# Queries' scores in partition order, the last chunk's stores from two queues, and a list order made anew, in a pack-attention and two-layer kernel on one Trainium2 core

## The chip, the core and the metric

The kernel runs on one core of a Trainium2 chip (trn2). The core has five engines that work side by side, each through its own list of instructions in order: TensorE (PE in the profile; PEld is its loading of weights), VectorE (DVE), ScalarE (ACT), GpSimd (POOL) and SyncE (SP), which here only issues DMA transfers. An engine that reaches an instruction whose input is not ready waits, and everything behind it in its list waits too. The metric is the device time of one execution in microseconds; less is better.

## The reference

Two attentions, then two dense layers. Inputs of the attention are q, k, v of shape (8 batches, 8 heads, 576 rows, 64) and p of shape (8, 8, 32, 64), float32.

```python
def sm_attn(qq, kk, vv):
    s = scale * np.matmul(qq, kk.transpose(0, 1, 3, 2))
    s = s - np.max(s, axis=-1, keepdims=True)
    a = np.exp(s)
    a = a / (np.sum(a, axis=-1, keepdims=True) + 1e-09)
    return np.matmul(a, vv)
p_packed = sm_attn(p, k, v)
x = sm_attn(q, p_packed, p_packed)      # then to (4608 tokens, 512)
# first layer (w_in 512x2048, w_out 2048x512, float64)
h = x @ w_in
P = a[0] + a[1] * h + a[2] * h**2 + a[3] * h**3
Q = 1.0 + abs(b[0]) * abs(h) + abs(b[1]) * h**2
x = ((P / (Q + 1e-6)) @ w_out).astype(np.float32)
# second layer, with its own w_in and w_out
h = x @ w_in
out = ((h * np.cos(h)) @ w_out).astype(np.float32)
```

The four weight matrices come as float64.

## The kernel before

**Attention.** The work is cut into 16 units u, one batch and four heads each. For each unit SyncE loads p, k, q and v (`load`); TensorE transposes k and q (`trans`), makes the first scores (`scores` with k = 0, L497), and after `max1`, `exp1`, `turn_exp` and `pack` the second scores, those of the queries against the packed rows (`scores` with k = 1). The second softmax runs on VectorE, GpSimd and ScalarE: `turn2` (a transpose, L581), `max2`, `less_max2`, `exp2`, `sum2`, `recip2`, `scaled2`, `turn_back` (L608). `keep_attn` (L611) stores the unit's result, the tile a2T, to DRAM from SyncE. A query's row number is 18 x partition + column; `of_head` reads the transposed columns, and for the queries it permutes them (index j, a), so that the tokens of a unit stand in blocks of 96 rows. `store` undoes this permutation at the very end through `cols_of`.

**First layer.** 128 items j, in 16 chunks of 8 items; a chunk c is 288 tokens. Ahead of each chunk its operand is loaded from DRAM (`a2_load`, SyncE), rounded to a high half (`a2_hi`, ScalarE, L684) and a low half (`a2_lo`, GpSimd, L687): the float32 products are made of three products of such halves. `m_load` and `m_prod` (L691) merge the packed rows with w_in into the operand M of a batch, split by `m_hi` (ScalarE) and `m_lo` (VectorE). An item is `front` (12 matmuls, L733, rows L743), the rational function in ten steps on ScalarE, VectorE and GpSimd (`absolute`, `lin`, `slope`, two `cubic` (L854, L856), `denom` on GpSimd (L866, rows L868), `rsqrt`, `square`, `over`, `ratio`), the splitting of its result into gh (`upper`, ScalarE) and gl (`lower`, VectorE), and `back` (L764, rows L780), four pieces that add into the accumulators.

**Second layer.** 144 items in 9 chunks of 512 tokens with 16 items each, the same shape with a cosine in place of the rational function. Its weights are converted while the first layer runs. At a chunk's end `done2` (L794) copies the four accumulator tiles out, two on ScalarE and two on VectorE, and `store` (L801) sends each tile to DRAM in four stores of 32 rows of 2 KB, all issued by SyncE.

**Weights.** float64 is turned into float32 by bit operations (`convert`, L405): `w_load` on SyncE into one of two buffers called raw, `w_exp` and `w_low` on ScalarE (L362), `w_abs` and `w_join` on VectorE (L381), and for most a split `w_hi` (ScalarE) and `w_lo` (GpSimd, L393). `w_in` of the first layer comes in 16 slabs f, `w_load(0, f, i)`; `m_prod` reads slabs 0 to 7 for its first half and 8 to 15 for its second.

**What sets the order.** No instruction's place is written by hand. While the program is built, the class Plan gets every step with an engine, an estimated duration and a key (about the time at which it should run), shifted by the number for its kind in the table WANTED. `Plan.order` (L118) walks through a made-up time, lets DMA transfers share one bus of RATE bytes per ns, and picks on each engine the step with the least key among those that could begin soon. The list that results for each engine is then fixed (`manual_schedule`). The keys of the attention come from FROM + u x UNIT, those of the first layer's conversions from a line in the item number. So one number in these tables can move instructions on every engine.

Of the kernel before, what the change touches and what calls it, by code (L numbers as in the profile page):

```python
# [27 lines left out]
class Plan:  # L28
# [11 lines left out]
    WINDOW = 60  # L40

    WANTED = {
        "a2_hi": 425, "a2_lo": 322, "a2_load": -80, "absolute": -759, "back 0": 65, "back 1": 130,
        "clipped": 158, "copied k": 134, "copied q": -49, "cosine": 272, "cubic 0": 306,
        "cubic 1": -373, "denom": -204, "done1": -251, "done2": -15, "doubled": 206, "exp1": 136,
        "exp2": -30, "exp_copied 0": -90, "exp_copied 1": 531, "front 0": -349, "front 1": -353,
        "keep_attn": 269, "keep_out": 130, "keep_pack": 152, "less_max2": -482, "lin 0": -197,
        "lin 1": -324, "load k": 278, "load p": -295, "load q": -297, "load v": 153, "lower 0": -68,
        "lower 1": 31, "m_hi": -104, "m_lo": -5, "m_load": -283, "m_prod": -385, "max1": -518,
        "max2": -130, "open_left": -238, "open_right": 397, "over 0": 48, "over 1": 82, "pack": 387,  # L50
        "packed": -296, "ratio": 12, "recip1": 167, "recip2": 132, "reduced 0": 243,
        "reduced 1": -199, "rounded": 269, "rsqrt": 244, "scaled2": 33, "scores 0": -163,
        "scores 1": 165, "slope": -174, "square": -374, "store": 310, "sum2": -42, "taken p": -65,
        "taken pp": 152, "times": -67, "trans k": 216, "trans q": 121, "turn2": 62,
        "turn_back": -264, "turn_exp": 97, "turned p": 95, "turned pp": 513, "upper 0": -254,
# [6 lines left out]
        "x_load": -108, "x_out": -463,  # L62
    }
    RATE = 275.0
    SHARED = ("over", "ratio", "lower", "rounded", "clipped", "w_abs", "w_join", "x_lo")

    def __init__(self, slots, mixed):
# [134 lines left out]
def pack_attention_moe_moe_kernel(  # L202
# [14 lines left out]
    nc = tc.nc  # L217
    B, H, S, D = q.shape
# [3 lines left out]
    P = 128  # L222
    KC = DM // P
    NF = FF // P
    CH = 512
    NCH = NT // CH
    TP = 96
    TCN = S // TP
    HS = S // 2
    N3 = TCN // 2  # L230
    NJ = TP // 32
    NT9 = S // 64
    G4 = 4
# [75 lines left out]
    add = plan.add  # L309
    TILE = {}  # L310
# [13 lines left out]
    par = POOL["cp"].tile([P, 8], F32, name="par")  # L324
    cst = POOL["cp"].tile([P, 4], F32, name="cst")

    def cols_of(i):
        return 2 * (i % N3) + i // N3

    def halves_of(t):  # L330
        return t[:, 0:CH], t[:, CH : 2 * CH]

# [143 lines left out]
        t0, t1 = PIECES[j]  # L476
        nc.scalar.copy(TILE[nm + "T", u][:, t0 * P : t1 * P], piece(u, nm, j))

    def of_head(t, h, k):

        if k == 0:
            return t.rearrange("q (t h p) -> q t h p", t=NT9, h=G4)[:, :, h, :]
        return t.rearrange("q (j a h p) -> q a j h p", j=NJ, a=N3, h=G4)[:, :, :, h, :]

    def doubled(u):
        t = TILE["p", u]
# [10 lines left out]
    def scores(u, k, lhs, rhs):  # L497

        for e in range(2):
            rows = slice(e * D, (e + 1) * D)  # L500
            for h in range(G4):
                r = slice(h * NP, (h + 1) * NP)
                nc.tensor.matmul(  # L503
                    TILE["s", u, k][r, e, 0:HS],
                    lhsT=TILE[lhs, u][rows, r],
                    rhs=of_head(TILE[rhs, u][rows], h, k),
                    start=True,
                    stop=True,
                )
# [101 lines left out]
    def keep_attn(u):  # L611
        nc.sync.dma_start(a2[u], TILE["a2T", u])

    UNIT, FROM = 30.47, -351.0
    exps, ld_users, tp_users, ps_users = [], [], [], []

    def attention(u):
# [180 lines left out]
        else:  # L798
            nc.scalar.copy(ob, acc)

    def store(c, m):  # L801
        ob = TILE["o", c, m]
        a, e = c * CH + m * P, c * CH + (m + 1) * P
        while a < e:
            blk, p0 = divmod(a, TP)
            b, i = divmod(blk, TCN)
            jj, p0 = divmod(p0, 32)
            n = min(e - a, 32 - p0)
            rows = out[b * S : (b + 1) * S, :].rearrange("(p j c) d -> j p c d", j=NJ, c=TCN)
            o = a - (c * CH + m * P)  # L810
            nc.sync.dma_start(rows[jj, p0 : p0 + n, cols_of(i), :], ob[o : o + n, :])
            a += n

    def x_pieces(c):
        done = 0
# [126 lines left out]
    t = add("-", 0, 0, open_right, after=tp_users)  # L942
    OPEN |= dict.fromkeys(("gp", "op", "xp", "wo1", "aps"), t)

    for n in range(0, NF, NF // 2):
        for e, which in enumerate("io"):
            for f in range(n, n + NF // 2):
                convert(0, f, which, -1257.8 + 36.58 * (f + n + e * NF // 2))

    ps2 = ([P, 2, CH], F32)  # L950
    W2P = ([P, 2 * HS], F32)
# [2 lines left out]
    for f in range(NF // 2, NF):  # L954
        part, e = divmod(f - NF // 2, 2)
        a, g = divmod(part, NG)
# [67 lines left out]
    def item2(j):  # L1024
        l, c, f = items[j]
        key = at(j)
        fronts[j] = add("PE", 2775, key, front, j, tail=170, r=[("win2", f), *(("x", c, kk) for kk in range(KC))], new=[("b2", ("h", j), *ps2)], after=[fronts[j - 1]] if j else ())
        add("ACT", 520, key, lin, j, tail=100, r=[("h", j)], new=[("T", ("T", j), *W2P)])
        add("DVE", 336, key, rounded, j, tail=85, w=[("T", j)])
        add("DVE", 605, key, reduced, j, 0, tail=85, r=[("T", j), ("h", j)], new=[("U", ("U", j), *W2P)])  # L1030
        add("DVE", 605, key, reduced, j, 1, tail=85, r=[("T", j)], w=[("U", j)])
        add("DVE", 336, key, clipped, j, tail=85, w=[("U", j)])
        add("ACT", 535, key, cosine, j, tail=100, w=[("U", j)], after=rsqrts[-8:] if j < N1 + 8 else ())
        add("DVE", 600, key, times, j, tail=85, r=[("U", j), ("h", j)], new=[("V", ("V", j), *W2P)])
        add("ACT", 510, key, upper, j, tail=100, r=[("V", j)], new=[("gh", ("gh", j), [P, 2 * HS], F32R)])
        add("DVE", 600, key, lower, j, tail=85, r=[("V", j), ("gh", j)], new=[("gl", ("gl", j), [P, 2 * HS], F32R)])
        for m in range(KC):
            home = dict(w=[("acc", 1, c, m)]) if f else dict(new=[("acc", ("acc", 1, c, m), [P, CH], F32)])
            add("PE", 694, key, back, j, m, tail=170, r=[("gh", j), ("gl", j), ("wo", 1, f)], **home)
        if f == NF - 1:  # L1040
            for m in range(KC):
                add("DVE" if m % 2 else "ACT", 510 + 90 * (m % 2), key - 30, done2, c, m, tail=90, r=[("acc", 1, c, m)], new=[("sc" if m < 3 else "xr", ("o", c, m), [P, CH], F32)])
                add("SP", 300, key, store, c, m, r=[("o", c, m)], kb=256)

    KEEP1, KEEPN = 14, 6.2
    for c in range(NH):
# [69 lines left out]
```

## Time and profile before

| | us |
|---|---|
| median of three runs (1689.8 to 1692.67) | 1690.48 |
| the profiled execution | 1691.2 |
| its span | 1689.4 |
| TensorE busy (94% of the span) | 1579.6 |
| loading of weights, PEld (80%) | 1347.9 |
| VectorE busy (76%) | 1289.7 |
| ScalarE busy (60%) | 1020.5 |
| GpSimd busy (18%) | 310.4 |
| DMA queue q1, 119.06 MB | 23.9% of 16 engines' span |

The mean granted clock of TensorE was 0.972. The attention fills roughly the first 200 us, the first layer lasts until about 880 us and the second until the end. A busy share is a mean over these stages; where the time is lost has to be read stage by stage, from windows and from the timeline.

### The profile page before, as it was taken

What the parts mean: (1) busy time and instruction counts of PE and PEld (TensorE: products, weight loads), DVE (VectorE), ACT (ScalarE), POOL (GpSimd) and SP (SyncE); (2) the same over time, 40 slices, a digit from 0 to 9 for tenths busy, and PEclk for the clock granted to TensorE, in tenths of its full rate; (3) what the DMA queues carried; (4) which work ended last, traced back from release to release, by engine and by line L of the source; (5) the groups of instructions that cost most, each with busy time, mean ns of one, the idle gap of its engine ahead of it and who ended that gap; (6) DMA issues with size and microseconds to landing.
All of it is one profiled execution on the core that took longest, in us unless ns stands there. A gap on an engine that the chain in (4) does not pass through costs nothing.

```text
span 1689.4 us, 26694 instructions
## 1 busy us (share of the span) xinstructions
PE 1579.6 (94%) x10176; PEld 1347.9 (80%) x10176; DVE 1289.7 (76%) x2025; ACT 1020.5 (60%) x1706; POOL 310.4 (18%) x246
## 2 busy tenths in 40 slices
PE   5766488999999999999999999999999999999997
PEld 3444287999998999998998888888888888888886
DVE  2656888999988999989998866666676757576664
ACT  4656788989889999979886533333333333343332
POOL 0233333324333433333322100000000000000000
PEclk7988789999999999999999999999999999999999
DMA  9997431211211211213153210101010101001011
GB/s 262 252 285 223 123 106 44 66 50 53 69 47 56 66 50 53 69 47 134 55 185 86 79 44 7 38 13 38 13 38 11 36 5 31 20 17 34 1 25 26
DMA packets 84384, 120.76 MB, mean 71 GB/s; under 512 B 19232, under 2 KB 61216, under 8 KB 84256
## 3 DMA queue, kind: packets, MB, share of 16 engines
q1 hardware_dynamic: 84256, 119.06, 23.9%
q8 instruction: 80, 1.31, 0.3%
q14 instruction: 48, 0.39, 0.1%
HBM read 85.99 MB, written 33.03 MB: 70 GB/s over the span
## 4 chain that ended last, share of the span: by engine, by line
PE 79%; DVE 7%; ACT 7%; DMA 2%; issue 2%; POOL 1%; SPq 0%; ACTq 0%; POOLq 0%; DVEq 0%
PE acc L780 42%; PE b L759 24%; PE b L743 9%; PE b L471 1%; PE b L698 1%; PE b L503 1%; DMA v_in<-in_v_dram 1%; ACT T L845 1%; ACT V L859 1%; DVE T L879 1%; DVE T L854 1%; DVE U L879 1%; DVE gl L914 1%; PE one L554 1%; DVE T L856 1%
## 5 line engine op out<-in xcount | busy, mean ns | idle before, releaser
L780 PE MATMUL acc<-gh,wo 128*128 128x288 f32 x2048 | 418.2, 298 | 14.3 <-ACT gh L911 14.3
L780 PE MATMUL acc<-wo,gh 128*128 128x512 f32 x1152 | 359.1, 393 | 0.0
L780 PEld LDWEIGHTS acc<-gh,wo 128*128 128x128 f32 x2048 | 331.4, 189 | 33.1 <-ACT gh L911 18.9
L780 PE MATMUL acc<-gl,wo 128*128 128x288 f32 x1024 | 304.9, 298 | 6.9 <-DVE gl L914 6.8
L780 PEld LDWEIGHTS acc<-wo,gh 128*128 128x128 f32 x1152 | 216.2, 188 | 49.3
L868 POOL TENSOR_TENSOR U<-U,V 128x576 f32<-128x576 f32 x128 | 183.4, 1442 | 367.3 <-DVE T L883 76.8
L780 PE MATMUL acc<-wo,gl 128*128 128x512 f32 x576 | 226.6, 393 | 0.0
L902 ACT ACTIVATE U<-U 128x512 f32<-128x512 f32 x144 | 90.7, 630 | 196.0 <-DVE U L898 195.8
L780 PEld LDWEIGHTS acc<-gl,wo 128*128 128x128 f32 x1024 | 193.9, 189 | 8.9 <-DVE gl L914 8.9
L914 DVE TENSOR_TENSOR gl<-V,gh 128x512 fp32r<-128x512 f32 x144 | 100.0, 695 | 132.2 <-PE acc L780 131.0
L847 ACT ACTIVATE T<-b 128x512 f32<-128x512 f32 x144 | 85.9, 596 | 189.8 <-PE b L759 189.2
L911 ACT CAST gh<-V 128x512 fp32r<-128x512 f32 x144 | 89.3, 620 | 79.6 <-PE acc L780 76.8
L780 PEld LDWEIGHTS acc<-wo,gl 128*128 128x128 f32 x576 | 108.1, 188 | 24.9
L887 DVE TENSOR_SCALAR T<-T 128x512 f32<-128x512 f32 x144 | 62.2, 432 | 79.0 <-ACT T L847 78.9
L914 DVE TENSOR_TENSOR gl<-T,gh 128x576 fp32r<-128x576 f32 x128 | 106.6, 836 | 10.2 <-PE acc L780 4.3
L905 DVE TENSOR_TENSOR V<-U,b 128x512 f32<-128x512 f32 x144 | 98.4, 683 | 18.2 <-ACT U L902 14.3
L879 DVE SCALAR_TENSOR_TENSOR T<-T,par,V 128x576 f32<-128x576 f32 x128 | 104.8, 834 | 8.8 <-ACT V L875 8.5
L862 ACT ACTIVATE U<-V,par 128x576 f32<-128x576 f32 x128 | 110.9, 872 | 0.2
L845 ACT ACTIVATE T<-b,par 128x576 f32<-128x576 f32 x128 | 106.1, 834 | 2.1 <-DVE gl L914 1.7
L894 DVE SCALAR_TENSOR_TENSOR U<-T,U 128x512 f32<-128x512 f32 x144 | 103.5, 719 | 4.0
L854 DVE TENSOR_TENSOR T<-T,b 128x576 f32<-128x576 f32 x128 | 93.7, 745 | 16.5 <-ACT T L845 14.9
L856 DVE SCALAR_TENSOR_TENSOR T<-T,par,b 128x576 f32<-128x576 f32 x128 | 101.8, 810 | 3.9 <-ACT V L859 1.4
(182 smaller groups left out, 3055.8 us busy)
## 6 DMA issues: line engine op xcount, KB each, us to landing
raw<-in_moe_w_out_dram SPq DMA_DIRECT2D x32, 512.0 KB, 3.7
q_in<-in_q_dram SPq DMA_DIRECT2D x16, 576.0 KB, 5.2
k_in<-in_k_dram SPq DMA_DIRECT2D x16, 576.0 KB, 6.8
x<-ob SPq DMA_DIRECT2D x16, 576.0 KB, 3.4
raw<-in_moe_w_in_dram SPq DMA_DIRECT2D x32, 256.0 KB, 4.3
v_in<-in_v_dram SPq DMA_DIRECT2D x64, 128.0 KB, 5.1
raw<-in_moe_w_in_dram SPq DMA_DIRECT2D x16, 512.0 KB, 4.1
w<-sc SPq DMA_DIRECT2D x32, 256.0 KB, 2.4
```

The lines of the kernel that those rows point to most:

```text
L743: nc.tensor.matmul(TILE["h", j][:, e, 0:HS], lhsT=w[:, o : o + P], rhs=x[:, g, :], start=n == 0, stop=n == 3 * NG - 1,)
L759: nc.tensor.matmul(h, lhsT=w[:, ks], rhs=x, start=n == 0, stop=n == 3 * KC - 1)
L780: nc.tensor.matmul(o, lhsT=w, rhs=x, start=i == 0 and n == 0, stop=i == last and n == len(todo) - 1,)
L845: nc.scalar.activation(T, hidden(j), AF.Identity, scale=par[:, 3:4], bias=par[:, 2:3])
L854: nc.vector.tensor_tensor(T, T, h, op=ALU.mult)
L856: nc.vector.scalar_tensor_tensor(T, T, par[:, 1:2], h, op0=ALU.add, op1=ALU.mult)
L862: nc.scalar.activation(shaped(j, "U"), shaped(j, "V"), AF.Identity, scale=par[:, 5:6], bias=par[:, 4:5])
L868: return nc.gpsimd.tensor_tensor(Q, Q, V, op=ALU.mult)
L879: return nc.vector.scalar_tensor_tensor(t, t, add_, shaped(j, "V"), op0=ALU.add, op1=ALU.mult)
L894: return nc.vector.scalar_tensor_tensor(Y, T, -C2, Y, op0=ALU.mult, op1=ALU.add)
L905: nc.vector.tensor_tensor(shaped(j, "V"), shaped(j, "U"), hidden(j), op=ALU.mult)
L914: return nc.vector.tensor_tensor(shaped(j, "gl"), result(j), shaped(j, "gh").bitcast(F32), op=ALU.subtract)
```

## The change

Four edits.

1. **Order.** The table WANTED gets new numbers for nearly all kinds, RATE goes from 275 to 262, the keys of the attention units become -291.5 + 18.35 u (from -351 + 30.47 u), and those of the first layer's conversions start earlier and stand closer together. The planner is charged 450 ns for each store that is issued (before: 300 for the four of a tile together).
2. **Queries in partition order.** `of_head` drops the permutation: queries are read with the pattern that the keys had.
3. **Stores.** `store` gives rows in the new order, still four stores of 32 rows of 2 KB for a tile, 18 rows apart in the output; `cols_of` goes.
4. **Last chunk.** In the last chunk pieces 0 and 1 of each tile are issued by SyncE, pieces 2 and 3 by ScalarE, behind the copies that ScalarE makes there.

```diff
-        "a2_hi": 425, "a2_lo": 322, "a2_load": -80, "absolute": -759, "back 0": 65, "back 1": 130,
+        "a2_hi": 440, "a2_lo": 373, "a2_load": -22, "absolute": -628, "back 0": 104, "back 1": 169,
...
-    RATE = 275.0
+    RATE = 262.0
...
-    def of_head(t, h, k):
-
-        if k == 0:
-            return t.rearrange("q (t h p) -> q t h p", t=NT9, h=G4)[:, :, h, :]
-        return t.rearrange("q (j a h p) -> q a j h p", j=NJ, a=N3, h=G4)[:, :, :, h, :]
+    def of_head(t, h):
+        return t.rearrange("q (t h p) -> q t h p", t=NT9, h=G4)[:, :, h, :]
...
-    UNIT, FROM = 30.47, -351.0
+    UNIT, FROM = 18.35, -291.5
...
-    def store(c, m):
-        ob = TILE["o", c, m]
-        a, e = c * CH + m * P, c * CH + (m + 1) * P
-        while a < e:
-            blk, p0 = divmod(a, TP)
-            b, i = divmod(blk, TCN)
-            jj, p0 = divmod(p0, 32)
-            n = min(e - a, 32 - p0)
-            rows = out[b * S : (b + 1) * S, :].rearrange("(p j c) d -> j p c d", j=NJ, c=TCN)
-            o = a - (c * CH + m * P)
-            nc.sync.dma_start(rows[jj, p0 : p0 + n, cols_of(i), :], ob[o : o + n, :])
-            a += n
+    def store(c, m, queue, pieces):
+
+        for n in pieces:
+            b, a = divmod(c * CH + m * P + n * 32, S)
+            e, t = divmod(a // 32, NT9)
+            rows = out[b * S : (b + 1) * S, :].rearrange("(p t e) d -> e t p d", t=NT9, e=2)
+            queue.dma_start(rows[e, t], TILE["o", c, m][32 * n : 32 * (n + 1), :])
...
-                convert(0, f, which, -1257.8 + 36.58 * (f + n + e * NF // 2))
+                convert(0, f, which, -1473.7 + 32.65 * (f + n + e * NF // 2))
...
-                add("SP", 300, key, store, c, m, r=[("o", c, m)], kb=256)
+                ends = ((nc.sync, (0, 1)), (nc.scalar, (2, 3))) if c == NCH - 1 else ((nc.sync, range(4)),)
+                for queue, pieces in ends:
+                    eng = "SP" if queue is nc.sync else "ACT"
+                    add(eng, 450 * len(pieces), key, store, c, m, queue, pieces, r=[("o", c, m)], kb=256)
```

What the new numbers do to the lists, at three places. In these rows a line is that of its own version of the kernel, and the number behind a tile's name is a running one.

First, GpSimd's list around the low half of chunk 7's operand (`a2_lo(7)`, the row that writes a_1). U<-U,V is `denom` of one item each; before, these are the items 53, 54, 55, then 56 and 57. Chunk 7 begins with item 56. sc<-sc,sc is `w_lo` of the second layer. Before:

```order
L868 TENSOR_TENSOR U_5745<-U_5745,V_5739 128x576
L393 TENSOR_TENSOR sc_5802<-sc_5629,sc_5674 128x512
L868 TENSOR_TENSOR U_5781<-U_5781,V_5754 128x576
L868 TENSOR_TENSOR U_5833<-U_5833,V_5813 128x576
L689 TENSOR_TENSOR a_1_5694<-xr_5436,a_1_5694 128x576
L868 TENSOR_TENSOR U_5978<-U_5978,V_5966 128x576
L868 TENSOR_TENSOR U_5999<-U_5999,V_5987 128x576
```

After, with the items 48, 49, then 50 and 51:

```order
L390 TENSOR_TENSOR sc_5400<-sc_5241,sc_5300 128x512
L857 TENSOR_TENSOR U_5449<-U_5449,V_5443 128x576
L857 TENSOR_TENSOR U_5485<-U_5485,V_5458 128x576
L683 TENSOR_TENSOR a_1_5508<-xr_5422,a_1_5508 128x576
L857 TENSOR_TENSOR U_5538<-U_5538,V_5516 128x576
L857 TENSOR_TENSOR U_5605<-U_5605,V_5556 128x576
```

The low half stood behind denom(55), one item ahead of its chunk; it now stands behind denom(49). a2_lo(13) moves in the same way, from behind denom(103) to behind denom(97).

Second, SyncE's list where the attention ends. raw<-in_moe_w_in_dram is `w_load` of one slab of the first layer's w_in, here slabs 10 to 15 in order; a<-a2T is `keep_attn`, here of units 13, 14 and 15; pt<-ppt is `m_load`. Before:

```order
L345 DMA raw_2328<-in_moe_w_in_dram 64x512 x2
L345 DMA raw_2369<-in_moe_w_in_dram 64x512 x2
L612 DMA a_13_85<-a2T_2367 128x576
L345 DMA raw_2436<-in_moe_w_in_dram 64x512 x2
L345 DMA raw_2443<-in_moe_w_in_dram 64x512 x2
L673 DMA pt_2460<-ppt_90 128x128
L345 DMA raw_2484<-in_moe_w_in_dram 64x512 x2
L345 DMA raw_2498<-in_moe_w_in_dram 64x512 x2
L612 DMA a_14_86<-a2T_2505 128x576
L612 DMA a_15_87<-a2T_2511 128x576
```

After:

```order
L342 DMA raw_2340<-in_moe_w_in_dram 64x512 x2
L606 DMA a_13_85<-a2T_2352 128x576
L606 DMA a_14_86<-a2T_2373 128x576
L342 DMA raw_2407<-in_moe_w_in_dram 64x512 x2
L342 DMA raw_2413<-in_moe_w_in_dram 64x512 x2
L342 DMA raw_2454<-in_moe_w_in_dram 64x512 x2
L667 DMA pt_2472<-ppt_90 128x128
L342 DMA raw_2479<-in_moe_w_in_dram 64x512 x2
L606 DMA a_15_87<-a2T_2484 128x576
L342 DMA raw_2520<-in_moe_w_in_dram 64x512 x2
```

The stores of the units 13 and 14 now stand ahead of slab 11, and that of unit 15 ahead of slab 15; before, the units 14 and 15 came behind the last slab.

Third, ScalarE's list at the end. sc<-acc is `done2` of the tiles 0 and 2. Before, it ends so:

```order
L902 ACTIVATE U_16643<-U_16643 128x512
L911 CAST gh_16674<-V_16638 128x512
L911 CAST gh_16690<-V_16664 128x512
L799 COPY sc_16721<-acc_16227 128x512
L799 COPY sc_16735<-acc_16245 128x512
```

After:

```order
L793 COPY sc_16721<-acc_16227 128x512
L801 DMA out_dram<-sc_16721 32x512 x2
L793 COPY sc_16737<-acc_16241 128x512
L801 DMA out_dram<-sc_16730 32x512 x2
L801 DMA out_dram<-sc_16737 32x512 x2
L801 DMA out_dram<-xr_16741 32x512 x2
```

ScalarE issues two of the four stores of every tile, and those of tile 0 stand between its two copies.

## Rows read from the trace of the kernel before

**Rows 1.** The page: busy tenths of TensorE and DMA in 40 slices.

```profile
PE   5766488999999999999999999999999999999997
DMA  9997431211211211213153210101010101001011
```

**Rows 2.** Windows: us, PE busy (instructions), PEld, DVE, ACT, POOL, PEclk, DMA, GB/s.

```profile
500.00:510.00 10.00, 9.36 (x70) 9.12 (x69) 6.81 (x8) 7.24 (x12) 4.49 (x3) 1.00 0.00 0
...
500.00:600.00 100.00, 95.88 (x753) 90.97 (x759) 91.07 (x124) 89.99 (x145) 36.75 (x26) 1.00 0.16 52
600.00:700.00 100.00, 100.00 (x808) 94.14 (x788) 96.20 (x131) 92.29 (x148) 36.15 (x26) 1.00 0.18 58
700.00:800.00 100.00, 97.21 (x762) 91.78 (x761) 92.13 (x124) 85.88 (x136) 33.52 (x24) 1.00 0.27 91
1500.00:1600.00 100.00, 100.00 (x435) 81.17 (x434) 66.28 (x115) 35.59 (x61) 0.00 (x0) 1.00 0.07 16
```

**Rows 3.** Timeline, chunks 7 and 13: start, duration, engine, operation, [idle before <- releaser].

```profile
479.40 0.70 ACT L685 CAST a<-xr 128x576 fp32r<-128x576 f32 x1
...
499.58 2.03 POOL L689 TENSOR_TENSOR a<-xr,a 128x576 fp32r<-128x576 f32 x1 [4.21 <-DVE U L879]
...
501.67 0.40 PE L743 MATMUL b<-a,m00h 128*128 128x288 f32 x1 [0.64 <-POOL a L689]
...
749.00 2.03 POOL L689 TENSOR_TENSOR a<-xr,a 128x576 fp32r<-128x576 f32 x1 [6.02 <-issue]
...
778.12 0.50 PE L743 MATMUL b<-a,m10h 128*128 128x288 f32 x2 [1.47 <-DVE T L856]
```

**Rows 4.** Timeline, from attention to the first layer: VectorE, ScalarE and TensorE.

```profile
185.81 0.77 DVE L581 STREAM_TRANSPOSE r<-b 128x576 f32<-128x576 f32 x1
...
189.21 0.66 ACT L362 ACTIVATE sc<-raw 128x512 f32<-128x512 f32 x1
...
207.06 0.85 PE L780 MATMUL acc<-gh,wo 128*128 128x288 f32 x2 [12.61 <-ACT gh L911]
...
211.06 1.43 DVE L914 TENSOR_TENSOR gl<-T,gh 128x576 fp32r<-128x576 f32 x2 [1.34 <-DMA a<-a2T]
...
211.88 0.61 PE L780 MATMUL acc<-gl,wo 128*128 128x288 f32 x1 [3.97 <-DVE gl L914]
```

**Rows 5.** Timeline, same stretch: SyncE's DMA issues (SPq), slab 15's join, m_prod(0,1,1).

```profile
178.59 5.11 SPq L345 DMA_DIRECT2D raw<-in_moe_w_in_dram  x4
...
183.75 0.58 SPq L612 DMA_DIRECT2D a<-a2T  x1
...
206.91 1.86 SPq L612 DMA_DIRECT2D a<-a2T  x2
...
213.68 0.68 DVE L381 SCALAR_TENSOR_TENSOR s<-raw,sc 128x512 uint32<-128x512 uint32 x1
...
217.10 1.09 PE L698 MATMUL b<-s,pt 64*32 64x512 f32 x16
```

**Rows 6.** The end: a window, the timeline, all store issues (ns: least/median/most).

```profile
1679.30:1682.30 3.00, 1.43 (x7) 0.85 (x5) 1.38 (x2) 0.60 (x2) 0.00 (x0) 1.00 0.45 107
...
1679.34 5.87 SPq L811 DMA_DIRECT2D out_dram<-sc  x12
...
1680.09 0.59 ACT L799 COPY sc<-acc 128x512 f32<-128x512 f32 x1 [0.77 <-PE acc L780]
...
1680.77 0.69 DVE L797 COPY xr<-acc 128x512 f32<-128x512 f32 x1 [0.67 <-PE acc L780]
...
1685.31 1.79 SPq L811 DMA_DIRECT2D out_dram<-xr  x4
...
L811 SPq DMA_DIRECT2D out_dram<-sc x108: 314/423/823, 982.6 to 1684.8; - x108
```

**Rows 7.** Line 503, the scores' matmuls of queries and keys (ns: least/median/most).

```profile
L503 PE MATMUL b<-qT,lhpp x16: 684/684/686, 145.6 to 146.2; 64*32 64x288 f32 x16
L503 PE MATMUL b<-kT,lhp x16: 684/684/684, 146.6 to 147.1; 64*32 64x288 f32 x16
```

More of the change, by code (lines that the diff above doesn't have):

```diff
@@ L42 @@
     WANTED = {
-        "a2_hi": 425, "a2_lo": 322, "a2_load": -80, "absolute": -759, "back 0": 65, "back 1": 130,
[L44 to L54, printed above, removed]
@@ L55 @@
-        "turn_back": -264, "turn_exp": 97, "turned p": 95, "turned pp": 513, "upper 0": -254,
[6 rows of a table removed]
-        "x_load": -108, "x_out": -463,
+        "a2_hi": 440, "a2_lo": 373, "a2_load": -22, "absolute": -628, "back 0": 104, "back 1": 169,
+        "clipped": 70, "copied k": 251, "copied q": 43, "cosine": 245, "cubic 0": 228,
+        "cubic 1": -452, "denom": -187, "done1": -328, "done2": -87, "doubled": 357, "exp1": 189,
+        "exp2": 14, "exp_copied 0": -32, "exp_copied 1": 522, "front 0": -261, "front 1": -372,
@@ new lines @@
+        "keep_attn": 271, "keep_out": 425, "keep_pack": 48, "less_max2": -596, "lin 0": -168,
+        "lin 1": -278, "load k": 275, "load p": -435, "load q": -220, "load v": 93, "lower 0": -109,
+        "lower 1": 78, "m_hi": -93, "m_lo": 32, "m_load": -254, "m_prod": -307, "max1": -559,
+        "max2": -95, "open_left": -187, "open_right": 541, "over 0": 72, "over 1": 202, "pack": 436,
+        "packed": -313, "ratio": -102, "recip1": 165, "recip2": 77, "reduced 0": 285,
+        "reduced 1": -222, "rounded": 209, "rsqrt": 308, "scaled2": 49, "scores 0": -225,
@@ L63 @@
+        "scores 1": 191, "slope": -116, "square": -380, "store": 355, "sum2": 21, "taken p": -208,
+        "taken pp": 108, "times": -128, "trans k": 275, "trans q": 147, "turn2": 46,
+        "turn_back": -404, "turn_exp": 79, "turned p": 64, "turned pp": 562, "upper 0": -141,
[6 rows of a table added]
+        "x_load": -33, "x_out": -508,
     }
-    RATE = 275.0
+    RATE = 262.0
     SHARED = ("over", "ratio", "lower", "rounded", "clipped", "w_abs", "w_join", "x_lo")
@@ L325, in pack_attention_moe_moe_kernel @@
     cst = POOL["cp"].tile([P, 4], F32, name="cst")
-    def cols_of(i):
-        return 2 * (i % N3) + i // N3
     def halves_of(t):
@@ L505, in scores @@
                     lhsT=TILE[lhs, u][rows, r],
-                    rhs=of_head(TILE[rhs, u][rows], h, k),
+                    rhs=of_head(TILE[rhs, u][rows], h),
                     start=True,
```

12 rows, old and new, of the table WANTED are left out of this document.

## The prediction

> **What bounds the kernel now.** Read first TensorE's busy row (PE) in the page's 40 slices, with the DMA row under it [rows 1]: TensorE is at 4 to 8 tenths for seven slices of 42 us, then at 9; the DMA engines are full for the first three only. Then the windows [rows 2]. From 1500 to 1600 us TensorE is busy 100.00 of 100 us: there the second layer is TensorE's alone, and no new list can shorten it. From 600 to 700 us, in the first layer, it is 100.00 too. But from 500 to 600 it is 95.88 and from 700 to 800 it is 97.21, with the same work: 4.12 and 2.79 us are lost. Last the timeline of the end: the last copy out of the accumulators starts at 1680.77 us, and the span ends at 1689.4. So three places can give time: the stretch before the first layer is full, two spots in it, and the end. What is gained in one passes through to the end, since the second layer only shifts.
>
> **The middle: two starved chunk borders.** Chunk 7 begins with front(56), which needs the low half of its attention operand, made by a2_lo(7) on GpSimd (POOL). Its input was ready early: a2_hi(7) ran on ScalarE (ACT) at 479.40. GpSimd made the low half at 499.58, some 19 us later, because a2_lo(7) stands between denom(55) and denom(56) in its list; front(56) went on at 501.67 after a wait of 0.64 for it [rows 3]. The price is not the 0.64 but what follows: no new item reached VectorE (DVE), busy only 6.81 us from 500 to 510 [rows 2], and TensorE paid when that gap came round to it. Chunk 13 shows the same: a2_lo(13) at 749.00, and TensorE without work for 1.47 us at 778.12 [rows 3]. In the new list a2_lo(7) stands after denom(49) and a2_lo(13) after denom(97), six items earlier each. As a second sign I counted in both lists how many items VectorE has begun (first cubic) and not finished when it splits item j's result (lower): before, it is down to the item itself at j = 3, 55, 103 and 127, now only at 127. And no a2_lo now stands fewer than three denoms ahead of its chunk; the chunks that start between 600 and 700 us had theirs four ahead and cost TensorE nothing [rows 2]. So I remove 4.12 + 2.79 = 6.91 us and leave 0.5 for small waits of another kind: **-6.4 us**. Bounds: -6.9, and 0 if TensorE then waits as much at other items.
>
> **The tail.** In the last chunk SyncE (SP) issues 16 stores of 64 KB, 12 in 5.87 us and 4 in 1.79, from 1679.34 to 1687.10 [rows 6]: 0.48 us apiece, with 0.42 the median of all such issues. The tiles were there long before: the last copy ends at 1680.77 + 0.69. So the issue of 16 instructions is the chain, and 2.3 us after it the span ends. Now SyncE issues two of each tile's four and ScalarE the other two. SyncE: 8 x 0.48 = 3.8 us from 1679.34 on, 1683.2. ScalarE: its two stores of tile 0 (to 1680.30) now stand in front of its copy of tile 2, which ran at 1680.09 [rows 6]; that copy slips by 0.2 us, to 1680.9 at its end; then six stores follow, 6 x 0.48 = 2.9, to 1683.8. The last issue ends at 1683.8 in place of 1687.1: -3.3. At 0.42 it is 1680.2, 1680.8, 1683.3: -3.8. I take **-3.6 us**. No row shows a store issued by ScalarE. Its issue could be as short as the shortest row, 0.31, for -4.4; or the two queues could hold each other up, and twice the issue time gives 0. I stay near the rows because the engines that move the bytes have room: they were busy 0.45 of the time from 1679.3 to 1682.3, with one queue feeding them [rows 6]; two ask for about 0.9.
> A page of the Trainium skill, "DMA: Bandwidth & Descriptors", speaks against this term: its section "Issuing engines are not separate DMA queues" says that issuing from several engines saves only the sequencer's time, usually small beside the transfer, and "Queues, rings and completion order" that the two queues have no descriptor generator of their own. The first does not fit here: 7.7 us of issue stand against 2.3 after it. By the second the term would be 0, if that generator is what takes the 0.42 us; no run here shows it yet.
>
> **The hand-over from attention to the first layer (150 to 220 us).** Before it the loads are the same bytes in almost the same order, with the DMA engines full [rows 1], so I give that part 0. What moves is the end of attention. TensorE has the last scores of units 14 and 15 earlier, and on VectorE turn_back(14) goes up 28 places and turn_back(15) nine, of about 0.7 us each. In the trace the first second product waits 3.97 us for gl, whose split started at 211.06, when the store of the last attention tile had landed, since that frees the memory [rows 4]. With turn_back(15) nine places (some 6 us) earlier that wait can go: -4.0. The wait of 12.61 us before it, for gh [rows 4], is not bought by this: ScalarE and VectorE are full of weight conversions there. Against it: m_lo(0,0,1), which front(0) needs, now stands behind turn2(14), max2(14) and sum2(13) on VectorE (three of about 0.75, as at 185.81: 2.2 us), and its m_hi behind three conversions and an exp2 on ScalarE (four of 0.66, as at 189.21: 2.6 us) [rows 4]. These run beside each other in part; I take +2.6. Net: **-1.4 us**. Bounds: -5 (the wait for gh shrinks as well) and +5 (the 2.6 counts twice, on the fronts and on the last exp2, for which every rsqrt waits).
>
> **What costs nothing.** The queries' scores now read their columns by the simpler pattern that the keys' scores have always used; both take 684 ns [rows 7], so 0. The stores are still four per tile, 32 rows of 2 KB with a step of 18 rows: 0. The planner's rate and its larger charge for a store only set the lists. The second layer's lists differ a little up to item 146, where the conversions of w_out stand up to two items later; each is still ahead of the product that needs it: 0.
>
> **Sum.** -6.4 - 3.6 - 1.4 = -11.4. The profiled execution took 1691.2 us, 1.8 over its span of 1689.4 and 0.7 over the median of the three timed runs, 1690.48. From its own time the sum gives 1679.8, from the median 1690.48 - 11.4 = **1679.1 us**, which I take.
>
> **Rivals.**
> 1. The second queue gives nothing, because the 0.42 us is spent in a part that both queues share. For it: nothing in the trace excludes it, since only SyncE ever issued. Against it: one instruction took 0.31 and another 0.82 us for the same 64 KB [rows 6], which looks more like the issuing engine than like a fixed work per store. Time: 1690.48 - 6.4 - 1.4 = 1682.7.
> 2. The starvation moves instead of going. VectorE is nearly as full as TensorE (91.07 of 100 us from 500 to 600 [rows 2]), so a new low point elsewhere could cost as much as the old two. For it: the new list has places where only two items are under way (j = 26, 35, 65, 97). Against it: so had the old (24, 49, 58, 68), with waits of half a microsecond at most. Time: 1690.48 - 3.6 - 1.4 = 1685.5.
> 3. Slower: SyncE's queue is held by keep_attn(14). This store of an attention tile now stands in front of the load of weight slab 11; before, it stood behind that of slab 15. SyncE waits in order. If turn_back(14) came as late as it did (its store was issued at 206.91), slab 11 would be issued at 206.9 in place of some 183.7, 23.2 us late, and slabs 12 to 15 behind it, two buffers at a time [rows 5]. The product m_prod(0,1,1) that needs them ran at 217.10, 2.7 us after their last join ended (213.68 + 0.68) [rows 5]; it would come 23.2 - 2.7 = 20.5 us later, and the first layer with it: 1690.48 - 6.4 - 3.6 + 20.5 = 1701.0. It makes the kernel slower from the point where turn_back(14) comes 2.7 + 6.4 + 3.6 = some 13 us after 183.7. Against it: turn_back(14) stands two places behind turn_back(13), whose store went out at 183.75 [rows 5], so I expect it before 190.
>
> **How the numbers follow.** Forecast (three terms within their bounds) 0.66, rival 1 0.08, rival 2 0.14, rival 3 or as large a loss in the hand-over 0.08, a larger gain than the bounds 0.04. A measurement of this kernel can tell about 0.2%, 3.4 us, from no change: the border is 1687.1. The forecast and rival 1 lie below it nearly whole, rival 2 with two thirds. Faster 0.82, same 0.10, slower 0.08. The range: the bounds are -6.9 to 0, -4.4 to 0, -5 to +5; not all at one end, I take 1673.5 (close to -6.9, -4.4 and -5) to 1686.5, which takes in rivals 1 and 2.
>
> **What would show it.** Middle: TensorE busy over 99 us from 500 to 600 and from 700 to 800, a2_lo(7) some 30 us ahead of front(56). Tail: the last stores on both queues end 2 to 3 us after the last copy. Hand-over: the wait for gl before the first second product gone, front(0) 2 to 3 us later, slab 11 issued before 190. The prediction is wrong if an issue takes twice 0.42 us with both queues at work, if VectorE has a new stretch below 8 tenths between 300 and 870, or if slab 11 waits behind keep_attn(14).

## The result and the profile after

The changed kernel took 1676.55 us (median of four runs, 1674.88 to 1678.16) against 1690.8 for the kernel before on the same chip: ratio 0.9918, 95% interval [0.9906, 0.9931], so 13.9 us less (11.7 to 15.9). Timed once more beside the later experiments it took 1678.58 against 1690.11: ratio 0.9936 [0.9923, 0.9950], 10.8 us less (8.5 to 13.0). It is faster, by 0.8% and by 0.6%; 1679.1 was forecast, and the range held both medians.

The page of the changed kernel (span 1675.9 us), busy tenths in 40 slices, to be laid beside [rows 1]:

```profile
PE   4776579999999999999999999999999999999998
...
DMA  8998431211211121213242210101010101101010
```

The first seven slices look much as before. The windows, columns as in [rows 2]:

```profile
500.00:600.00 100.00, 100.00 (x800) 94.76 (x799) 97.65 (x128) 90.00 (x144) 35.40 (x26) 1.00 0.18 57
600.00:700.00 100.00, 100.00 (x797) 94.61 (x796) 96.87 (x132) 91.72 (x146) 36.38 (x26) 1.00 0.17 56
700.00:800.00 100.00, 99.84 (x779) 95.80 (x778) 95.09 (x127) 88.97 (x142) 35.47 (x26) 1.00 0.27 88
```

TensorE is full in both windows that had lost time, and VectorE went from 91.07 to 97.65 and from 92.13 to 95.09. TensorE's waits from 300 to 892 us (who waited, for what: total us, times, longest), first before:

```profile
PE b L743 <- DVE T L856: 2.9, 2, 1.5
PE acc L780 <- ACT gh L911: 1.4, 2, 1.2
PE b L743 <- POOL a L689: 1.3, 2, 0.7
PE acc L780 <- DVE gl L914: 1.1, 3, 0.5
PE b L759 <- DVE V L905: 0.6, 1, 0.6
PE b L698 <- DVE T L856: 0.3, 1, 0.3
```

and after, all that is left:

```profile
PE b L737 <- DVE T L845: 0.2, 1, 0.2
```

7.6 us of waits became 0.2. The end of the changed kernel, timeline (start, duration; SPq and ACTq are the issues of each queue), beside [rows 6]:

```profile
1669.60 2.71 SPq L801 DMA_DIRECT2D out_dram<-sc  x6
1669.60 0.86 ACTq L801 DMA_DIRECT2D out_dram<-sc  x2
...
1670.58 0.59 ACT L793 COPY sc<-acc 128x512 f32<-128x512 f32 x1 [1.01 <-PE acc L774]
...
1670.66 1.75 ACTq L801 DMA_DIRECT2D out_dram<-sc  x4
1671.03 0.69 DVE L791 COPY xr<-acc 128x512 f32<-128x512 f32 x1 [0.67 <-PE acc L774]
1672.49 0.79 SPq L801 DMA_DIRECT2D out_dram<-xr  x2
1672.67 0.79 ACTq L801 DMA_DIRECT2D out_dram<-xr  x2
```

The last issue ends at 1673.46, 1.74 us after the last copy; before it was 5.64 after it. With both queues at work a single store took 0.32 to 0.45 us to issue, in the median 0.37 on SyncE and 0.41 on ScalarE.

And the hand-over, beside [rows 4] and [rows 5]; L588 is exp2, here of unit 15:

```profile
185.14 1.70 SPq L606 DMA_DIRECT2D a<-a2T  x2
190.49 9.42 SPq L342 DMA_DIRECT2D raw<-in_moe_w_in_dram  x6
...
195.54 0.66 ACT L359 ACTIVATE sc<-raw 128x512 f32<-128x512 f32 x1 [0.94 <-DMA raw<-in_moe_w_in_dram]
...
196.65 0.67 ACT L588 ACTIVATE r<-r 128x576 f32<-128x576 f32 x1
...
209.70 0.85 PE L774 MATMUL acc<-gh,wo 128*128 128x288 f32 x2 [8.96 <-ACT gh L900]
211.27 0.61 PE L774 MATMUL acc<-gl,wo 128*128 128x288 f32 x1 [0.72 <-DVE gl L903]
```

The wait for gl fell from 3.97 to 0.72, but the first second product came at 209.70 in place of 207.06.

**Where the time went.** Three marks cut every trace: the end of chunk 0 (done1's first copy, 262.32 before and 262.23 after), the first copy of the last chunk (1678.73 and 1668.99; the expectations below call the stretch between these two "from chunk 0's end to the last copy") and the span's end.

| kernel | chunk 0 ends | from there to the last chunk's first copy | tail |
|---|---|---|---|
| before | 262.32 | 1416.41 | 10.67 |
| before, two queues (e1) | 260.99 | 1416.36 | 7.65 |
| e2_lo_early | 260.37 | 1416.89 | 10.74 |
| e2b_lo_front | 258.77 | 1416.46 | 10.37 |
| e3_all_lists | 261.90 | 1417.21 | 10.29 |
| e11_denom_too | 258.95 | 1418.18 | 10.27 |
| e12_one_key | 267.01 | 1409.59 | 6.90 |
| after | 262.23 | 1406.76 | 6.91 |
| after again (e13) | 260.62 | 1406.22 | 6.96 |
| after, one queue (e4) | 260.05 | 1406.77 | 10.28 |
| e9_merged | 265.91 | 1406.71 | 23.88 |
| e10_exp2_early | 263.95 | 1406.49 | 7.06 |
| e7_dve_more | 263.55 | 1412.11 | 7.04 |
| e8_pe_more | 262.17 | 1413.13 | 6.80 |

With the same list the middle column repeats within 0.6 us, while the first differs by up to 6 us. So the middle (-9.65) and the tail (-3.5: mean 10.44 of the five old lists and e4 on one queue, 6.95 on two in six traces, e1 and e9 left out) can be read from single traces, and the stretch up to chunk 0 cannot: there six traces with the old list end chunk 0 at 260.6 on average (258.8 to 262.3), six with the new one at 262.4 (260.1 to 265.9). That is +1.9 with an uncertainty of about 1. The sum, -9.65 - 3.5 + 1.9 = -11.3, agrees with the second timing and lies just short of the first's interval.

### The profile page after: what moved, and what is told of

It reads as the page before. It is cut to its first block, busy times and chain, and to the rows that moved or that the text cites. A ratio compares the mean times of both kernels' runs of the same rounds, so it can differ in the third digit from the quotient of the medians.

```text
span 1675.9 us, 26699 instructions
## 1 busy us (share of the span) xinstructions
PE 1581.6 (94%) x10176; PEld 1347.9 (80%) x10176; DVE 1289.6 (77%) x2025; ACT 1021.1 (61%) x1706; POOL 308.3 (18%) x246
## 4 chain that ended last, share of the span: by engine, by line
PE 86%; DMA 4%; DVE 4%; ACT 3%; issue 1%; POOL 1%; SPq 1%; POOLq 0%; ACTq 0%
PE acc L774 46%; PE b L753 24%; PE b L737 11%; PE b L692 2%; DMA raw<-in_moe_w_in_dram 1%; PE b L468 1%; PE b L497 1%; DMA v_in<-in_v_dram 1%; DMA raw<-in_moe_w_out_dram 1%; ACT sc L362 0%; DVE T L868 0%; ACT sc L359 0%; DVE U L868 0%; ACT e L515 0%; DMA q_in<-in_q_dram 0%
## 5 line engine op out<-in xcount | busy, mean ns | idle before, releaser
L774 PEld LDWEIGHTS acc<-gh,wo 128*128 128x128 f32 x2048 | 332.0, 190 | 26.9 <-issue 15.9
L903 DVE TENSOR_TENSOR gl<-T,gh 128x576 fp32r<-128x576 f32 x128 | 111.8, 876 | 7.4 <-PE acc L774 4.7
L848 ACT ACTIVATE V<-b 128x576 f32<-128x576 f32 x128 | 83.2, 651 | 35.1 <-PE b L737 26.0
```

What stands on the lines that cost most here:

```text
L774: nc.tensor.matmul(o, lhsT=w, rhs=x, start=i == 0 and n == 0, stop=i == last and n == len(todo) - 1,)
L903: return nc.vector.tensor_tensor(shaped(j, "gl"), result(j), shaped(j, "gh").bitcast(F32), op=ALU.subtract)
```

## The experiments

All edits that move a step use one helper, which takes it out of the planner's list and puts it right behind another; for GpSimd it also renews the VectorE instruction that the step is told to wait for:

```diff
-    for s in plan.order():
+    done = plan.order()
+    def move(name, args, to, to_args):
+        s, t = (next(x for x in done if (x.fn.__name__, x.args) == y) for y in ((name, args), (to, to_args)))
+        done.remove(s)
+        i = done.index(t) + 1
+        done.insert(i, s)
+        if s.port and s.eng == "POOL":
+            s.behind = next(x for x in reversed(done[:i]) if x.port and x.eng == "DVE")
...
+    for s in done:
```

### The tail: one queue or two

**e1_two_queues**, on the kernel before (its store takes a queue and the numbers of the pieces to issue):

```diff
-                add("SP", 300, key, store, c, m, r=[("o", c, m)], kb=256)
+                if c < NCH - 1:
+                    add("SP", 300, key, store, c, m, r=[("o", c, m)], kb=256)
+                else:
+                    add("SP", 900, key, store, c, m, nc.sync, (0, 1), r=[("o", c, m)], kb=256)
+                    add("ACT", 900, key, store, c, m, nc.scalar, (2, 3), r=[("o", c, m)], kb=256)
```

> The kernel before, with the last chunk's sixteen stores shared by SyncE and ScalarE and nothing else changed. Theory of the tail (the issue of the stores is the chain): 3.6 us less than before, about 1686.9, and the last issue some 3.3 us after the last copy begins. Rival (the rest of the new list is needed for it, or both queues hold each other up): within 1 us of before.

Measured: 1686.21 against 1688.86, ratio 0.9985 [0.9976, 0.9994], 2.5 us less (1.0 to 4.1); its tail 7.65 in place of 10.67.

**e4_one_queue**, on the changed kernel:

```diff
-                ends = ((nc.sync, (0, 1)), (nc.scalar, (2, 3))) if c == NCH - 1 else ((nc.sync, range(4)),)
+                ends = ((nc.sync, range(4)),)
```

> The changed kernel, with all sixteen stores of the last chunk issued by SyncE again. Theory of the tail: 3.7 us more than the changed kernel, about 1680.3. Rival (the gain at the end comes from the new place of the copies, not from the second queue): within 1 us of the changed kernel, 1676.5.

Measured: 1681.82, ratio to before 0.9956 [0.9942, 0.9971]; its tail 10.28, 3.4 more than after. Both runs say the same: the second queue alone is worth 3.0 to 3.4 us of the tail, in either list.

**e9_merged**, on the changed kernel:

```diff
+        if c == NCH - 1:
+            n = pieces[0]
+            while n <= pieces[-1]:
+                b, a = divmod(c * CH + m * P + n * 32, S)
+                e, t = divmod(a // 32, NT9)
+                k = min(pieces[-1] + 1 - n, NT9 - t)
+                rows = out[b * S : (b + 1) * S, :].rearrange("(p t e) d -> e t p d", t=NT9, e=2)
+                queue.dma_start(rows[e, t : t + k], TILE["o", c, m][32 * n : 32 * (n + k), :])
+                n += k
+            return
```

> The changed kernel, with the two stores that a queue issues for a tile of the last chunk made one where their rows follow each other in the output (half a tile each, 128 KB; tile 1's second half stays two). Theory of the tail (the issue of each store, about 0.44 us, is the chain on each queue): the last issue ends 0.8 to 1.2 us earlier after the last copy, the time is 1 us less than the changed kernel. Rival (the issue time goes with the bytes, or the landing of larger stores takes longer): within 0.4 us of the changed kernel, or slower.

Measured: 1696.55, ratio 1.0044 [1.0031, 1.0057] to before; the tail took 23.88. The theory falls, and the rival, which allowed for slower, had nothing of this size. A window of its end, columns as in [rows 2]:

```profile
1676.00:1694.00 18.00, 0.00 (x0) 0.00 (x0) 0.00 (x0) 0.00 (x0) 0.00 (x0) 0.57 0.17 53
```

For 18 us nothing ran but the stores, at 53 GB/s with 0.17 of the 16 DMA engines busy; in the changed kernel the end moved 210 GB/s with 0.74 busy (1669.5 to 1674.5). The merged store's outermost index has the value 2 (2 x 32 rows x 512), that of a single one 32. The Trainium skill, "DMA: Bandwidth & Descriptors", section "Why a DMA increments its semaphore by 16 and not by 1", says that a transfer uses the largest number of engines up to 16 that divides the slowest dimension of both its sides, so 2 here and 16 there. The trace agrees: from 1680 to 1692 us the busy share was 0.13, which is 2 of 16. The last of ScalarE's stores was also issued late, at 1684.77, 8.7 us behind the one before it; what held it is not shown.

### The middle: is it the late low half?

**e2_lo_early**, on the kernel before:

```diff
+    move("a2_lo", (7,), "denom", (52,))
+    move("a2_lo", (13,), "denom", (97,))
```

> The kernel before, with a2_lo(7) moved up in GpSimd's list from behind denom(55) to behind denom(52), and a2_lo(13) from behind denom(103) to behind denom(97). Theory of the prediction (the late low halves starve the two chunk borders): 6 to 10 us less, 1681 to 1684. Rival (the place of front(56) in TensorE's list, behind back(53, 3), is what starves it, since front(56) waited only 0.64 us for the low half): at most 1.5 us less, and front(56) still begins at about 500.7.

Measured: ratio 0.9998 [0.9990, 1.0007]; from chunk 6's end to chunk 8's 85.27 us (before 85.28), from chunk 12's to 13's 47.76 (47.77). The low half was made at 479.07 in place of 499.58, and front(56) no longer waited for it, but it began no earlier, 0.9 us later when counted from chunk 0's end. The prediction's theory falls here.

**e2b_lo_front**: as e2, and

```diff
+    move("front", (56,), "back", (50, 3))
+    move("front", (104,), "back", (98, 3))
```

> As the run with the low halves early, and also front(56) moved up in TensorE's list from behind back(53, 3) to behind back(50, 3), and front(104) from behind back(101, 3) to behind back(98, 3). Theory of the prediction: no more than the run with the low halves alone, within 1 us. Rival (the front's place): 6 to 10 us less than before, 1681 to 1684, while the low halves alone give almost nothing.

Measured: ratio 0.9999 [0.9990, 1.0007]; 85.29 and 47.75, although front(56) began 9.1 us earlier. The rival falls too.

**e3_all_lists**: as e2b, and for items 56 and 57 (104 and 105 alike)

```diff
+    move("front", (57,), "back", (51, 3))
+    move("absolute", (56,), "square", (55,))
+    move("lin", (56,), "absolute", (56,))
+    move("slope", (56,), "lin", (56,))
+    move("absolute", (57,), "upper", (54,))
+    move("lin", (57,), "absolute", (57,))
+    move("slope", (57,), "lin", (57,))
+    move("cubic", (56, 0), "over", (55, 1))
+    move("cubic", (56, 1), "ratio", (55,))
+    move("cubic", (57, 0), "lower", (54,))
+    move("cubic", (57, 1), "lower", (55,))
```

> The kernel before, with the first two items of chunk 7 (56, 57) and of chunk 13 (104, 105) moved up in every list: the low half on GpSimd and the two fronts on TensorE (as in the run before it), and also absolute, lin and slope on ScalarE and both cubics on VectorE, about as the changed kernel has them. Theory now (the starvation is real, but the old order had written the gap into the lists of all engines, so that moving the low half or the front alone buys nothing): the stretch from chunk 6's end to chunk 8's is 3 to 5.5 us shorter than before, and that from chunk 12's end to chunk 13's the same; the total 6 to 10 us less than before. Rival (the gain between chunks 5 and 14 comes from other places of the new order): each of the two stretches within 1 us of before.

Measured: ratio 1.0002 [0.9993, 1.0011]; 85.27 and 47.75. Its timeline showed one thing left to take away: denom(56) waited for lower(55), to which the planner had tied it, though its input was there at 499.6.

```profile
505.59 2.83 POOL L868 TENSOR_TENSOR U<-U,V 128x576 f32<-128x576 f32 x2 [9.45 <-DVE gl L914]
...
508.91 0.82 DVE L879 SCALAR_TENSOR_TENSOR T<-T,par,V 128x576 f32<-128x576 f32 x1 [2.66 <-ACT V L875]
...
523.96 0.53 PE L780 MATMUL acc<-gh,wo 128*128 128x288 f32 x2 [1.22 <-ACT gh L911]
...
550.98 0.51 PE L743 MATMUL b<-a,m00h 128*128 128x288 f32 x2 [1.44 <-DVE T L856]
```

**e11_denom_too**: as e3, and (104 alike)

```diff
+    move("denom", (56,), "slope", (56,))
+    move("denom", (57,), "slope", (57,))
+    move("rsqrt", (56,), "slope", (57,))
+    move("square", (56,), "rsqrt", (56,))
```

> As the run with items 56, 57, 104 and 105 moved up in all lists, and also their denom (with the wait for a VectorE instruction that the planner ties to each of GpSimd's) and the first of each pair's rsqrt and square. In that run denom(56) idled 9.45 us until lower(55) was done, though its input was ready. Theory (that explicit wait kept the gap): VectorE's wait of 2.66 us at 508.91 goes, and the stretch from chunk 6's end to chunk 8's is 2 to 4 us shorter than before's 85.28. Rival: within 1 us of 85.28.

Measured (one run): 1689.17; the stretches 86.47 and 47.60. That the first is 1.2 us longer goes with the clock, not with the list: behind TensorE's wait at 520 us the granted clock fell to its lower level (1.2 GHz) for 3.4 us, 0.66 on average from 520 to 525; in the trace of before it stays at 1.00 there. TensorE's idle time was the same (table below). The same spots in its timeline, whose times run 3.6 us ahead of e3's at chunk 6:

```profile
496.07 2.60 POOL L868 TENSOR_TENSOR U<-U,V 128x576 f32<-128x576 f32 x1 [3.53 <-DVE T L879]
...
520.35 0.53 PE L780 MATMUL acc<-gh,wo 128*128 128x288 f32 x2 [1.22 <-ACT gh L911]
...
548.60 0.50 PE L743 MATMUL b<-a,m00h 128*128 128x288 f32 x2 [1.44 <-DVE T L856]
```

denom(56) came 6 us earlier and VectorE's long wait for V went, and still TensorE waited 1.22 and 1.44 us at the same two instructions. So these two waits do not hang on VectorE's wait for V at chunk 7's border. But VectorE's gap as a whole was only shifted, never removed. Its idle time from 38 us ahead of chunk 6's end to chunk 8's end:

| kernel | VectorE idle, us | TensorE idle, us |
|---|---|---|
| before | 10.1 | 4.1 |
| e2_lo_early | 10.1 | 4.2 |
| e2b_lo_front | 10.8 | 4.2 |
| e3_all_lists | 11.1 | 4.2 |
| e11_denom_too | 10.6 | 4.1 |
| e12_one_key (below) | 5.5 | 0.9 |
| after | 3.5 | 0.0 |

Whether TensorE's waits come from VectorE's idle time is therefore not shown by these runs; the two fall together.

**e12_one_key**, on the kernel before, with e1's edit of the stores and

```diff
-        "a2_hi": 425, "a2_lo": 322, "a2_load": -80, "absolute": -759, "back 0": 65, "back 1": 130,
+        "a2_hi": 425, "a2_lo": -250, "a2_load": -80, "absolute": -759, "back 0": 65, "back 1": 130,
```

> The kernel before with two edits: the planner's number for a2_lo is -250 instead of 322, so that the whole order is planned anew with every low half at least five items ahead of its chunk from chunk 1 on, and the last chunk's stores go from two queues. Table, rate and attention keys are otherwise the old ones. Theory (the late low half is the root, and the planner had written the gap behind it into the lists of all engines): from chunk 0's end to the last copy 8 to 10 us less than the 1416.4 of before, about 1407.5; with 3.0 to 3.8 from the tail and the attention as before the total is 11 to 13 us less than before. Rival (the gain of the new order has other sources than a2_lo): that stretch within 3 us of 1416.4, the total 3 to 6 us less than before.

Measured: 1686.13, ratio 0.9976 [0.9967, 0.9984], 4.1 us less (2.7 to 5.6); 1409.59 for the middle. Of its -6.8 there, 3.4 fall between chunk 0 and chunk 1 and go with a chunk 0 that ended later (267.01); from chunk 1's end on it gains 3.5, where the changed kernel gains 12.4. Both figures hold work that is only done earlier: between the ends of chunk 0 and chunk 1 TensorE runs 96 front matmuls before, 108 here and 120 in the changed kernel, at 0.133 us each, which is 1.6 and 3.2 us. Some 1.9 and 9.2 are left. Its waits of TensorE from 300 to 892 us:

```profile
PE acc L780 <- DVE gl L917: 1.6, 3, 0.5
PE b L698 <- DVE T L859: 0.8, 2, 0.4
PE b L743 <- ACT V L862: 0.8, 3, 0.3
PE b L743 <- DVE T L859: 0.7, 3, 0.3
```

Half of the waits went (7.6 to 3.9). The stretch lies between theory and rival, the total in the rival's range: a new order with early low halves is worth some, less than a third of what the new table gives. Its waits fell by more than its time did, so the listed waits are not the whole price.

### What lost time costs in the full stretch

**e7_dve_more** and **e8_pe_more**, each on the changed kernel:

```diff
     def lower(j):
-        return nc.vector.tensor_tensor(
-            shaped(j, "gl"), result(j), shaped(j, "gh").bitcast(F32), op=ALU.subtract
-        )
+        for _ in range(2 if 72 <= j < 80 else 1):
+            t = nc.vector.tensor_tensor(
+                shaped(j, "gl"), result(j), shaped(j, "gh").bitcast(F32), op=ALU.subtract
+            )
+        return t
```

```diff
-    def front(j):
+    def front(j, again=False):
+        if j in (72, 74, 76, 78) and not again:
+            front(j, True)
```

> The changed kernel, with lower done twice for the items 72 to 79 (the same result): 8 x 0.84 = 6.7 us more of VectorE's time in the full stretch of the first layer. Theory (VectorE is as full there as TensorE, so time that it loses is never made up): chunk 9's end comes 5 to 7 us later and stays so to the end. Rival (TensorE alone is the bound, VectorE has room): at most 2 us later.

> The changed kernel, with front done twice for the items 72, 74, 76 and 78 (the same result): 4 x 1.6 = 6.4 us more of TensorE's time in the full stretch of the first layer. The same amount of VectorE's time cost 5.5 us of 6.7. Theory (both engines are full there): chunk 9's end, against chunk 8's, comes 5 to 6.5 us later than in the changed kernel and stays so. Rival (VectorE alone is the bound): at most 2 us later.

Measured (one run each): 6.7 us more of VectorE's time lengthened the middle by 5.35 (1412.11 against 1406.76), 6.4 us more of TensorE's time by 6.37 (1413.13), half of it before chunk 8's end, since the fronts run ahead. Neither was made up later. Both engines set the pace in that stretch of the first layer.

### The hand-over

**e10_exp2_early**, on the changed kernel, the moves that matter (of 23):

```diff
+    move("max2", (15,), "turn2", (15,))
+    move("less_max2", (15,), "max2", (15,))
+    move("exp2", (15,), "slope", (2,))
+    move("rsqrt", (0,), "exp2", (15,))
+    move("square", (0,), "rsqrt", (0,))
...
+    move("sum2", (15,), "cubic", (2, 1))
...
+    move("turn_back", (15,), "over", (0, 1))
+    move("keep_attn", (15,), "turn_back", (15,))
+    move("open_right", (), "keep_attn", (15,))
+    move("ratio", (0,), "cubic", (3, 1))
+    move("upper", (0,), "w_low", (0, 11, 'i'))
```

> The changed kernel, with the end of unit 15's second softmax (max2, less_max2, exp2, sum2, recip2, scaled2, turn_back, its store) and the rational function of items 0 and 1 moved up in the lists of ScalarE, VectorE, GpSimd and SyncE. Theory (in the changed kernel the last exp2, at 196.65 us, holds every rsqrt and so the first second product, which came at 209.70): the first second product comes 3 to 6 us earlier, and chunk 0 ends 2 to 5 us earlier, the total as much. Rival (VectorE and TensorE are full there, or the weights' loads set it): chunk 1's end within 1.5 us of the changed kernel.

Measured: 1680.59, ratio 0.9951 [0.9937, 0.9964] to before, so 8.3 us less than before (6.1 to 10.6), no better than the changed kernel. Counted from front(0), the first second product came after 27.4 us in place of 32.4, as the theory has it, but chunk 0 ended after 88.8 in place of 85.0. TensorE's waits from 195 to 265 us say who took it:

```profile
PE b L692 <- DVE s L378: 10.7, 3, 5.4
PE b L737 <- ACT V L848: 5.7, 1, 5.7
```

L692 is m_prod, which waits for the last joins of the weights; in the changed kernel it waited 3.7 there. Chunk 1's end came 139.1 us after front(0), in place of 135.4. The theory falls; the rival, which allowed 1.5 us either way, is nearer.

**e13_after_again**: the changed kernel as it is.

> The changed kernel unchanged, on the same chip as the other runs of this group, for its time beside them. Theory: from chunk 0's end to the last copy 1406.8 as in its first trace, the tail 6.9, and only the time up to chunk 0's end different (260 to 266 us in the traces with this list, 259 to 262 with the old one), so 10 to 13 us less than before. Rival (the attention's end is faster in the new list too): 14 us or more less than before.

Measured: as told above, 1678.58 and 10.8 us less than before; the theory's figures hold.

## Why the prediction was right, and where it was not

**The total** (-11.4) was right, 13.9 and 10.8 measured, but that it fits is luck: the middle gave 3.25 us more than forecast and the hand-over 3.3 less, and the two cancelled.

**The tail** (-3.6) was right, in size and cause: -3.5 by the marks, and it comes and goes with the second queue alone (e1, e4). Rival 1 is out: with both queues at work a store took 0.32 to 0.45 us to issue, no more than with one. By the Trainium skill, "DMA: Bandwidth & Descriptors", section "Issuing engines are not separate DMA queues", a second queue only saves issue time; the runs agree, but here the issue was the longer part, 7.7 us against 2.3. A limit in the part that both queues share, which the forecast weighed, did not show.

**The middle** (-6.4) had the right place and the right sign, a wrong cause and too small a size: -9.65, beyond its bound of -6.9. The step that failed is "The price is not the 0.64 but what follows", which makes the late low half the cause of VectorE's gap, and has TensorE pay "when that gap came round to it". The first link is refuted. Taking the late low half away bought 0.0 (e2), with the front 0.0 (e2b), with all lists nothing (e3) and with denom nothing (e11), and VectorE's idle time there stayed at 10.1 to 11.1 us, TensorE's 1.22 and 1.44 with it. The second link is open: no move took VectorE's idle time away. The second sign falls too: in e3 and e11 three items were under way on VectorE at j = 55 and at 103 (one before; three and four in the changed kernel), and nothing was gained. Planning the whole order anew with early low halves got some 1.9 of 9.2 from chunk 1 on (e12). What is shown: the waits of TensorE between 300 and 892 us went from 7.6 to 0.2, VectorE's idle time around chunk 7 from 10.1 to 3.5, and time lost in the stretch of chunk 9 by VectorE or TensorE is not made up (e7, e8). Which of the moved instructions does it stays open; that it is many of them together was only argued, from the failure of the single ones.

The size: the forecast took the idle time of two windows, 6.91. Between the two marks TensorE's idle time went from 11.6 to 3.3 us, 8.3 less: 6.75 in those two windows and 1.55 outside them. The other 1.35 of the 9.65 is no idle time in the traces. TensorE counts as busy for that much less between the marks, with as many matmuls, and why is not shown.

**The hand-over** (-1.4) had the wrong sign: about +1.9, within the bounds. Both of its booked terms came. From the first product with gh to the first with gl it took 4.82 us before and 1.57 after: 3.25 of the 4.0. And m_lo(0,0,1) began 6.5 us later than with the old list, on average of six traces each, 2.3 more than front(0) itself: most of the 2.6. What failed is the step ahead of them, "so I give that part 0": front(0) began at 177.2 on average, 4.2 later, and this delay is older than the hand-over. The ninth turn2 already started at 126.4 (123.7 to 129.8) in place of 122.0 (121.1 to 123.0). Which of the new keys does that is not shown.

The first second product moved with front(0), 32.4 us after it in the first trace of either kernel, since the last exp2 ran at 196.65 in place of 190.01, behind conversions whose slab SyncE loaded at 190.49; e10 took 5 us out of this stretch and lost them again by chunk 0's end. SyncE was not held by keep_attn(14), the second of the two issues from 185.14 to 186.84 (rival 3 did not come). It went on right behind the join of slab 9, the first of two in the 1.28 us from 189.74, which frees one of the two buffers for slabs; the forecast "slab 11 before 190" missed by 0.5.

**What costs nothing**: the queries' scores took 427 ns in the median, as the keys' did (403 and 483 before, both while the granted clock changed, between 0.61 and 1.00 in windows of 20 us); nothing shows a cost. **Rival 2** did not come: no window of 100 us between 300 and 900 us has VectorE below 94.

## What to carry to other kernels

A chain of short DMA issues at the end of a kernel is worth splitting over two queues, but not worth merging before one has seen what the outermost index of the merged transfer is. In lists that a planner has written, an instruction that is visibly late need not be what costs the time: move it alone first (e2 is two lines), and price the stretch only then, by all engines that are full there. And compare traces from a mark behind the part that varies from run to run: here everything after chunk 1 repeats within some 0.1 us for a given list, everything before it only within several. Between two lists the mark must also have the same work behind it: two fronts done earlier looked like 3.2 us gained.

## What the runs showed of the hardware that was not expected

A store of 64 rows of 2 KB whose outermost index has the value 2 kept 0.17 of the DMA engines busy and made the tail 23.88 us in place of 6.91, although it moved the same bytes in fewer instructions. Two queues that issue at the same time did not slow each other: 0.37 us a store on SyncE and 0.41 on ScalarE (medians of the last chunk), against 0.42 on SyncE alone before. One wait of TensorE of 1.22 us (e11) was followed by 3.4 us at the lower granted clock; the same wait in e3 was not.
